# Three-slot W2 items, output projections beside attention, and queue-jumping W1 items in a fused attention and MLP kernel

## The chip, the core and the metric

The kernel runs on one core of one Trainium2 chip. The metric is device time in microseconds (us) of one execution. One timed execution varies by a few us from run to run, so times are given as medians.

The engines have short names in the profile: PE is TensorE (matmuls), PEld its weight loads, DVE is VectorE, ACT is ScalarE, SP is the engine that issues the DMAs. "L316" is line 316 of the kernel that was run; the change shifts lines, so the same statement has another number after.

## The reference, cut to what matters

```python
x  = A_x                                   # (1, 2048, 1024) bf16
xn = layernorm(x)
s  = attention(xn, A_wqkv) @ A_wo          # 32 heads of 32
y  = layernorm(xn)
h  = gelu(y @ B_w1 + B_b1)                 # (2048, 3584), tanh form of gelu
g  = silu(h @ B_w2 + B_b2)
return x + s * g
```

## The kernel before

The kernel records all operations first, with the keys that each reads and writes, and then emits one in-order stream for each engine, with a semaphore wait wherever an operation needs another engine's result. So the order in which Python records operations is the order in which an engine must execute them.

The frame is 512 "attention units": a unit is one block of 256 queries against 256 keys for four heads. In each unit ScalarE does two exponentials over 128 x 1024 values. Beside the unit TensorE runs one slot of other work, an "item", in the one PSUM bank (bank 7) that attention leaves free:

- W: a W1 item, 128 hidden features of one token chunk: 32 matmuls of 352 columns (288 in the last of six chunks),
- 2: a slot of a W2 item. A W2 item has 112 matmuls and is cut in four slots of 28,
- q, v: projections for the next head group: 32 matmuls,
- o: an output-projection item: 32 matmuls. There are 48, and what does not fit beside attention runs after it.

A W1 item gives VectorE four operations: the eviction of the bank with the bias (to `xb`), then square and cube, and, after a tanh on ScalarE for two items at once, a "gate" that writes `hT`, the input of W2. Only the eviction is recorded at once. The others stand in a list `dq`, from which each unit takes as many as a budget allows:

```python
        def later(cost, fn, lag=1):
            dq.append((cur["u"] + lag, cost, fn))

        def run_dq(budget, limit=None):     # takes from the front what fits the budget
            ...
        def hurry(cond):                    # empties the list from the front until cond holds
            while not cond():
                for v in sorted(act_tasks):
                    for t in act_tasks.pop(v):
                        t()
                run_dq(1e9, 1)

        def take(*keys):                    # a buffer is wanted again
            hurry(lambda: not busy.intersection(keys))
            busy.update(keys)
...
        # w1_item, when its matmuls are recorded (cut)
                take(kx, ku)
                op("vector", ... tensor_scalar(xb, bank(bk), b1T[:, f], op0=ALU.add), r=[("b", bk), "b1"], w=[kx])
                def square(): ...; later(0.45, cube)
                def cube():   ...; act_tasks[cur["u"] + 1].append(tanh)     # for the second of a pair
                def tanh():
                    take(kt)
                    op("scalar", ... activation(th, ut, ACT.Tanh), r=kus, w=[kt])
                    for i, (xq, kq, fq) in enumerate(pairs[m2]):
                        later(0.45, lambda ...: gate(i, xq, kq, fq), lag=0)
                def gate(i, xq, kq, fq): ...                                # hT[:, fq] = (th + 1) * xb
                    have.add((c, fq))
                later(0.45, square)
...
        # w2_item, one step: four matmuls on hT[:, f]
            def step(f, bk):
                hurry(lambda: (c, f) in have)
                op("tensor", ..., r=[("war", s, f // 4), ("hT", f)], w=[("b", bk)])
...
        NXB, NUB, NTH = 6, 2, 2      # buffers for xb, u (pairs), th (pairs)
        BUDGET = 1.25
        # the loop over units (cut)
            if u < NU: s_unit(u); exp_unit(u)        # scores, exponentials
            if 2 <= u < NU + 2: pv_unit(u - 2)       # PV and row sums
            ... the item of this unit ...
            room = BUDGET - (0.8 if ended else 0.0)
            room -= run_dq(room)
            if hi == len(it.steps):
                it.finish(state["bank"])             # records the eviction
```

`hurry` flushes the list. When a W2 slot is recorded whose `hT` is not yet produced, or when a buffer is wanted that a waiting gate still reads, everything in front of it in the list goes into VectorE's stream at that point, and the next operation of that stream waits until all of it has run.

The softmax here doesn't subtract the row's maximum and nothing guards it: scores larger than these inputs give would overflow.

Of the kernel before, what the change touches and what calls it, by code (L numbers as in the profile page):

```python
# [6 lines left out]
ACT = mybir.ActivationFunctionType  # L7
# [112 lines left out]
def bass_recurrent_scan__mha_block__mixer_channel_mlp__prompt_kernel(  # L120
# [14 lines left out]
    DC = D // 128  # L135
# [23 lines left out]
    with ExitStack() as st:  # L159
# [10 lines left out]
        iota_i = sb("iota_i", [128, 128], I32)  # L170
# [7 lines left out]
        accs = [sb(f"accs{i}", [128, QW], F32) for i in range(2)]  # L178
        trs = [sb(f"trs{i}", [128, QW], F32) for i in range(2)]
        r8s = [sb(f"r8s{i}", [128, QW // 32], F32) for i in range(2)]  # L180
        rcs = [sb(f"rcs{i}", [128, QW], F32) for i in range(2)]
# [4 lines left out]
        NXB, NUB, NTH = 6, 2, 2  # L186
        xb_t = [sb(f"xb{i}", [128, CW], F32) for i in range(NXB)]
        u_t = [sb(f"u{i}", [128, 2, CW], F32) for i in range(NUB)]
        th_t = [sb(f"th{i}", [128, 2, CW], F32) for i in range(NTH)]
# [52 lines left out]
        op("gpsimd", lambda e: e.iota(iota_i[:], pattern=[[1, 128]], base=0, channel_multiplier=-1), w=["iota"])  # L242
        op("gpsimd", lambda e: e.memset(mhalf[:], -0.5), w=["mhalf"])
        op("vector", lambda e: e.tensor_single_scalar(ident[:], iota_i[:], 0, op=ALU.is_equal), r=["iota"], w=["ident"])
# [116 lines left out]
        def later(cost, fn, lag=1):  # L361

            dq.append((cur["u"] + lag, cost, fn))

        def run_dq(budget, limit=None):
            done = 0.0
            i = 0
            while i < len(dq):
                first, cost, fn = dq[i]
                if (limit is None and first > cur["u"]) or done + cost > budget:  # L370
                    i += 1
                    if done + 0.1 > budget:
                        break
                    continue
                dq.pop(i)
                done += cost
                fn()
                if limit is not None:
                    break
            return done  # L380

        def hurry(cond):

            while not cond():
                for v in sorted(act_tasks):
                    for t in act_tasks.pop(v):
                        t()
                run_dq(1e9, 1)
# [5 lines left out]
        cur = {"u": 0}  # L394
# [37 lines left out]
        def w1_item(c, f):  # L432
# [14 lines left out]
            def fin(bk):  # L447
# [3 lines left out]
                xb, ut, th = xb_t[m % NXB], u_t[m2 % NUB], th_t[m2 % NTH]  # L451
                ub = ut[:, h, :]
                kx, ku, kt = ("xb", m % NXB), ("ub", m2 % NUB, h), ("th", m2 % NTH)
# [6 lines left out]
                def square():  # L460
                    op("vector", lambda e: e.tensor_tensor(ub[:, 0:n], xb[:, 0:n], xb[:, 0:n], op=ALU.mult), r=[kx], w=[ku])  # L461
                    later(0.45, cube)
# [8 lines left out]
                def tanh():  # L471
                    take(kt)
                    op("scalar", lambda e: e.activation(th[:, :, 0:n], ut[:, :, 0:n], ACT.Tanh, scale=0.7978845608028654 * 0.044715),  # L473
                       r=kus, w=[kt])
                    busy.difference_update(kus)
                    for i, (xq, kq, fq) in enumerate(pairs[m2]):
                        later(0.45, lambda i=i, xq=xq, kq=kq, fq=fq: gate(i, xq, kq, fq), lag=0)

                def gate(i, xq, kq, fq):
                    op("vector", lambda e: e.scalar_tensor_tensor(hT[:, fq, 0:n], th[:, i, 0:n], 1.0, xq[:, 0:n], op0=ALU.add, op1=ALU.mult),  # L480
                       r=[kt, kq], w=[("hT", fq)] + ([("xnb", i) for i in range(4)] if c == 0 else []))
                    busy.discard(kq)
                    if i == 1:
                        busy.discard(kt)
                    have.add((c, fq))
                later(0.45, square)
# [4 lines left out]
        def w2_item(c, nb):  # L491
# [36 lines left out]
            return Item([lambda bk, f=f: step(f, bk) for f in range(FB)], fin, parts=4, pre=pre)  # L528
# [3 lines left out]
        def load_res(tb):  # L532
            i4 = tb % NTB
            op("sync", lambda e: e.dma_start(xres[i4], x2[tb * 128:(tb + 1) * 128, :]), w=[("xres", i4)], dma=f"rx{i4}",
               after=[tail["xfree"]])
            lo, hi = tb * 128, (tb + 1) * 128
            cs = [c for c, (t0, n) in enumerate(chunks) if t0 < hi and t0 + n > lo]
            op("sync", lambda e: e.dma_start_transpose(gres[i4].rearrange("p (a n) -> p a n", a=1), gT_d[:, lo:hi]),
               r=[("gT", nb, c) for nb in range(DC) for c in cs], w=[("gres", i4)], dma=f"rg{i4}", after=[tail["xfree"]])
# [104 lines left out]
        for c in range(NCH):  # L644
            for f in range(FB):
                mlp.append([(w1_item(c, f), 0, DC)])
            for nb in range(DC):
                it = w2_item(c, nb)
                q = FB // it.parts
                mlp.append([(it, p * q, (p + 1) * q) for p in range(it.parts)])  # L650
# [3 lines left out]
        for hg in range(HG - 1):  # L654
# [26 lines left out]
            while len(flat) < end:  # L681
# [3 lines left out]
                if need and len(flat) >= first_proj and (late or credit >= 1):  # L685
# [15 lines left out]
        tails = mlp[mi:]  # L701
        for x in tails:
            flat += x
        for tb in range(NT):
            for k in range(len(ncol)):
                flat.append((wo_item(tb, k), 0, HG))
# [35 lines left out]
        def pv_unit(u):  # L742
# [17 lines left out]
            if kp == NKP - 1:  # L760
                g = cnt["g"]
                cnt["g"] += 1
                a, rc = accs[g % 2], rcs[g % 2]
                ka, kr = ("accs", g % 2), ("rcs", g % 2)
# [10 lines left out]
                def spread():  # L775
                    op("vector", lambda e: e.transpose(rc[:], r8[:].rearrange("p (b i) -> p b i", i=1).to_broadcast((128, QW // 32, 32))),
                       r=[kr8], w=[kr])
                    later(0.35, scale)

                def scale():  # L780
                    op("vector", lambda e: e.tensor_tensor(OT[:, hg, qb * QW:(qb + 1) * QW], a[:], rc[:], op=ALU.mult),
                       r=[ka, kr], w=[("OT", hg, qb), ("xst", 2 * hg), ("xst", 2 * hg + 1)])
                    busy.discard(ka)
                    scaled.add((hg, qb))
# [3 lines left out]
        BUDGET = 1.25  # L788
# [4 lines left out]
        while u < NU + 2 or state["qi"] < total or dq or act_tasks:  # L793
# [18 lines left out]
            if u >= NP and state["qi"] < total:  # L812
# [3 lines left out]
                it, lo, hi = entry  # L816
                for hp, which in loads.pop(qi, ()):
                    if hp < HG // 2:
                        load_wq(hp, which)
                if lo == 0:  # L820
                    if it.pre:
                        it.pre()
                    if u >= NU + 2:
                        state["bank"] = tail_banks[(tail_banks.index(state["bank"]) + 1) % len(tail_banks)]
                for fn, *a in sp_tasks.pop(u, ()):
                    fn(*a)
                for s in it.steps[lo:hi]:
                    s(state["bank"])
                room = BUDGET - (0.8 if ended else 0.0)
                room -= run_dq(room)  # L830
                if ys and (room > 0.5 or u >= 32):
                    ynorm(ys.pop(0))
                if hi == len(it.steps):
                    it.finish(state["bank"])
# [59 lines left out]
```

## Time and profile before

The median was 1132.98 us of three runs (1132.63 to 1133.45). What matters:

| | before |
|---|---|
| TensorE busy, ScalarE busy | 96%, 92% of the span |
| a unit with a W2 slot / with 32 matmuls (352 columns) | 1.92 us / 2.07 us |
| ScalarE's part of a unit | 1.83 us, and 0.57 us of tanh for two W1 items |
| TensorE waits for `hT` | 7.6 us (matmuls), 12.1 us (weight loads) |
| output projection after attention | 1088 matmuls, 39.6 us |

The first lines are from the page (busy us, share of the span, instructions), then from the waits (engine, line and tile that waited <- what it waited for: us in total, times, longest) and from the chain of waits that ended last (start us, us, what).

```profile
PE 1092.0 (96%) x29952; PEld 692.6 (61%) x29952; DVE 616.4 (54%) x1415; ACT 1046.6 (92%) x1197; POOL 24.0 (2%) x64
```
```profile
PEld ps L316 <- DVE hT L480: 12.1, 13, 2.6
PE ps L316 <- DVE hT L480: 7.6, 7, 2.3
```
```profile
953.97 10.40 DMA war<-in_B_w_dram
...
1089.44 39.61 PE ps L316 x1088
```

A matmul and its weight load wait for the same thing, so those two totals overlap and are not to be added. The DMA piece of 10.40 us is a load of MLP weights, where the median of these loads is 4.1 us. It was issued just after the 2 MB load of `wo`.

The timeline of TensorE (start us, us, engine, line, operation, tiles, count, and in brackets the idle time before and what ended it) shows an ordinary unit with a W2 slot of 28 matmuls. From one group of scores (L724) to the next it is 173.30 - 171.37 = 1.93 us:

```profile
171.37 0.40 PE L724 MATMUL ps<-QT,KT 32*128 32x256 bf16 x8
171.70 0.29 PE L753 MATMUL ps<-P,VP 128*32 128x256 bf16 x4
...
172.15 1.22 PE L316 MATMUL ps<-hT,war 128*32 128x352 bf16 x28
173.30 0.40 PE L724 MATMUL ps<-QT,KT 32*128 32x256 bf16 x8
```

Then the passage from W1 to W2 in chunk 4. The W2 slot stops after 20 matmuls for 2.19 us, until the last gates have written `hT`:

```profile
864.97 0.92 PE L316 MATMUL ps<-hT,war 128*32 128x352 bf16 x20
868.08 0.77 PE L316 MATMUL ps<-hT,war 128*32 128x352 bf16 x8 [2.19 <-DVE hT L480]
868.78 0.60 PE L724 MATMUL ps<-QT,KT 32*128 32x256 bf16 x8
...
870.14 2.25 PE L316 MATMUL ps<-hT,war 128*32 128x352 bf16 x28
872.33 0.40 PE L724 MATMUL ps<-QT,KT 32*128 32x256 bf16 x8
```

It is not VectorE that is full here. It stood idle for 4.00 us before these gates, because the tanh that they read came late on ScalarE, behind a row of exponentials:

```profile
861.14 5.66 ACT L736 ACTIVATE P<-ps 128x1024 bf16<-128x1024 f32 x6
866.56 0.91 ACT L473 ACTIVATE th<-u 128x704 f32<-128x704 f32 x1
867.50 0.96 DVE L480 SCALAR_TENSOR_TENSOR hT<-th,xb 128x352 bf16<-128x352 f32 x2 [4.00 <-ACT th L473]
```

The built order shows how the list leads there. The last two cubes were still in the list when the W2 slot was recorded, `hurry` then recorded the tanh after that unit's two exponentials, and the gates after the tanh. The stops near 164, 691 and 1004 us look the same.

The windows of one us (for each window the busy us of the engines, then the granted clock of TensorE, the DMA share and GB/s):

```profile
867.00:868.00 1.00, 0.00 (x0) 0.00 (x0) 0.50 (x2) 0.47 (x1) 0.00 (x0) 1.00 0.91 274
868.00:869.00 1.00, 0.81 (x16) 0.34 (x16) 0.56 (x3) 0.00 (x0) 0.00 (x0) 0.92 0.14 42
869.00:870.00 1.00, 1.00 (x24) 0.53 (x20) 0.49 (x1) 0.56 (x1) 0.00 (x0) 0.50 0.06 16
870.00:871.00 1.00, 1.00 (x20) 0.58 (x16) 0.00 (x0) 1.00 (x2) 0.00 (x0) 0.50 0.00 0
871.00:872.00 1.00, 1.00 (x20) 0.49 (x12) 0.15 (x1) 0.76 (x2) 0.00 (x0) 0.50 0.00 0
872.00:873.00 1.00, 1.00 (x30) 0.46 (x26) 0.37 (x1) 0.22 (x1) 0.00 (x0) 0.88 0.00 0
```

### The profile page before, as it was taken

To read this page: it belongs to the slowest core of one execution; us is meant where nothing else is said; L and a number is where in the kernel's file an instruction comes from. 1 tells how busy PE (TensorE), PEld (TensorE's weight loads), DVE (VectorE), ACT (ScalarE), POOL (GpSimd) and SP (SyncE) were. 2 spreads that over 40 slices of the span, in tenths; PEclk is the share of its full clock that TensorE was granted. 3 is DMA by queue.
4 is the path that set the end of the run, shared out by engine and by line. 5 is a ranking of instruction groups with operands and counts; after the bars stand their busy time and mean duration, and the time that the engine had idled before them with its cause. 6 is when DMAs were issued, how large, how long until landed. Compare 5 with 4: busy or idle time off the path is not lost.

```text
span 1133.6 us, 63287 instructions
## 1 busy us (share of the span) xinstructions
PE 1092.0 (96%) x29952; PEld 692.6 (61%) x29952; DVE 616.4 (54%) x1415; ACT 1046.6 (92%) x1197; POOL 24.0 (2%) x64
## 2 busy tenths in 40 slices
PE   5999999999999999999999999999999999989998
PEld 4856656666666666665566655666655665656666
DVE  8457862266663237774237663246574246842378
ACT  4899999999999999999999999999998999989930
POOL 4300000000000000000000000000000000000000
PEclk9999999999999999999999999999999999989999
DMA  9233545323316404324522327431234435534677
GB/s 233 68 105 110 185 112 164 115 62 97 96 40 156 128 23 138 106 78 115 144 89 78 105 77 173 127 96 48 78 105 110 120 95 167 160 92 125 118 174 170
DMA packets 202420, 129.93 MB, mean 115 GB/s; under 512 B 45488, under 2 KB 192944, under 8 KB 202160
## 3 DMA queue, kind: packets, MB, share of 16 engines
q1 hardware_dynamic: 197520, 125.86, 39.6%
q8 instruction: 234, 3.83, 1.4%
q0 software_dynamic: 4640, 0.02, 0.6%
q14 instruction: 26, 0.21, 0.1%
HBM read 104.87 MB, written 12.58 MB: 104 GB/s over the span
## 4 chain that ended last, share of the span: by engine, by line
PE 53%; ACT 42%; DVE 2%; DMA 2%; issue 1%; SPq 0%; POOL 0%; DVEq 0%
ACT P L736 37%; PE ps L316 31%; PE ps L724 9%; PE ps L753 8%; PE ps L756 5%; ACT th L473 4%; DMA war<-in_B_w_dram 1%; DVE stats L253 1%; DMA xnT<-gT_scratch 0%; PE ps L307 0%; DVE hT L480 0%; ACT thz L518 0%; DMA OT<-in_A_x_dram 0%; DVE wq L564 0%; DVE hT L285 0%
## 5 line engine op out<-in xcount | busy, mean ns | idle before, releaser
L736 ACT ACTIVATE P<-ps 128x1024 bf16<-128x1024 f32 x1024 | 967.6, 1076 | 21.1 <-PE ps L724 14.8
L753 PE MATMUL ps<-P,VP 128*32 128x256 bf16 x4096 | 262.9, 279 | 0.0
L756 PE MATMUL ps<-P,ones 128*32 128x256 bf16 x4096 | 257.8, 274 | 0.0
L316 PE MATMUL ps<-hT,war 128*32 128x352 bf16 (+1 forms) x5376 | 233.2, 311 | 9.5 <-DVE hT L480 7.6
L316 PE MATMUL ps<-yTc,war 128*32 128x352 bf16 (+1 forms) x5376 | 226.1, 309 | 3.0 <-issue 1.2
L724 PE MATMUL ps<-QT,KT 32*128 32x256 bf16 x4096 | 204.7, 274 | 12.9 <-ACT P L736 7.7
L753 PEld LDWEIGHTS ps<-P,VP 128*32 128x32 bf16 x4096 | 107.6, 95 | 111.1 <-issue 104.9
L316 PEld LDWEIGHTS ps<-hT,war 128*32 128x32 bf16 x5376 | 141.5, 98 | 54.8 <-DVE hT L480 11.3
L316 PEld LDWEIGHTS ps<-yTc,war 128*32 128x32 bf16 x5376 | 138.6, 97 | 50.0 <-issue 1.8
L455 DVE TENSOR_SCALAR xb<-ps,b1T 128x352 f32<-128x352 f32 (+1 forms) x168 | 96.2, 572 | 124.3 <-PE ps L316 124.1
L724 PEld LDWEIGHTS ps<-QT,KT 32*128 32x128 bf16 x4096 | 60.9, 92 | 157.8 <-ACT P L736 98.8
L316 PE MATMUL ps<-xnT,wq 128*32 128x352 bf16 (+2 forms) x3200 | 129.5, 305 | 2.6 <-DMA wq<-in_A_wqkv_dram 1.4
L756 PEld LDWEIGHTS ps<-P,ones 128*32 128x32 bf16 x4096 | 109.2, 96 | 1.3
L514 DVE TENSOR_SCALAR zh<-ps,b2h 128x352 f32<-128x352 f32 (+1 forms) x48 | 27.5, 573 | 137.6 <-PE ps L316 137.6
L316 PEld LDWEIGHTS ps<-xnT,wq 128*32 128x32 bf16 x3200 | 80.5, 97 | 30.2 <-DMA wq<-in_A_wqkv_dram 1.7
L480 DVE SCALAR_TENSOR_TENSOR hT<-th,xb 128x352 bf16<-128x352 f32 (+1 forms) x168 | 82.3, 505 | 24.8 <-ACT th L473 24.4
L465 DVE SCALAR_TENSOR_TENSOR u<-u,xb 128x352 f32<-128x352 f32 (+1 forms) x168 | 83.7, 504 | 0.0
L461 DVE TENSOR_TENSOR u<-xb 128x352 f32<-128x352 f32 (+1 forms) x168 | 83.4, 503 | 0.3
L768 DVE COPY accs<-ps 128x256 f32<-128x256 f32 x64 | 27.2, 424 | 78.4 <-PE ps L756 78.3
L473 ACT ACTIVATE th<-u 128x704 f32<-128x704 f32 (+1 forms) x84 | 67.7, 805 | 0.4 <-DVE u L465 0.4
L316 PE MATMUL ps<-wq,xnT 128*32 128x256 bf16 x2048 | 65.6, 273 | 0.9 <-DMA wq<-in_A_wqkv_dram 0.6
L316 PE MATMUL ps<-xnT,OT 128*32 128x352 bf16 (+1 forms) x1536 | 58.0, 308 | 0.5 <-DVE wq L564 0.5
(44 smaller groups left out, 463.5 us busy)
## 6 DMA issues: line engine op xcount, KB each, us to landing
war<-in_B_w_dram SPq DMA_DIRECT2D x336, 256.0 KB, 4.1
wq<-in_A_wqkv_dram SPq DMA_DIRECT2D x12, 512.0 KB, 4.9
OT<-in_A_x_dram SPq DMA_DIRECT2D x16, 256.0 KB, 7.6
y_scratch<-OT SPq DMA_DIRECT2D x16, 256.0 KB, 3.3
xnT<-in_A_x_dram SPq DMA_DIRECT2D x16, 256.0 KB, 4.2
out_dram<-wq SPq DMA_DIRECT2D x16, 256.0 KB, 2.6
gT_scratch<-gst SPq DMA_DIRECT2D x40, 88.0 KB, 1.7
xnT<-in_A_wo_dram SPq DMA_DIRECT2D x1, 2048.0 KB, 10.0
```

The costliest lines, as they stand in the source:

```text
L316: ins = e.matmul(outs(j), lhsT=lhs(j), rhs=rhs, start=start, stop=stop, tile_position=(0, 32 * j), skip_group_check=True)
L455: op("vector", lambda e: e.tensor_scalar(xb[:, 0:n], bank(bk, 0, n), b1T[:, f:f + 1], None, op0=ALU.add), r=[("b", bk), "b1"], w=[kx])
L461: op("vector", lambda e: e.tensor_tensor(ub[:, 0:n], xb[:, 0:n], xb[:, 0:n], op=ALU.mult), r=[kx], w=[ku])
L465: op("vector", lambda e: e.scalar_tensor_tensor(ub[:, 0:n], ub[:, 0:n], 1.0 / 0.044715, xb[:, 0:n], op0=ALU.add, op1=ALU.mult), r=[kx, ku] ...
L473: op("scalar", lambda e: e.activation(th[:, :, 0:n], ut[:, :, 0:n], ACT.Tanh, scale=0.7978845608028654 * 0.044715), r=kus, w=[kt])
L480: op("vector", lambda e: e.scalar_tensor_tensor(hT[:, fq, 0:n], th[:, i, 0:n], 1.0, xq[:, 0:n], op0=ALU.add, op1=ALU.mult), r=[kt, kq], w= ...
L514: op("vector", lambda e: e.tensor_scalar(zh[:, 0:n], bank(bk, 0, n), 0.25, b2h[:, nb:nb + 1], op0=ALU.mult, op1=ALU.add), r=[("b", bk), "b ...
L724: ins = e.matmul(bank(bks[j], kh * 256, (kh + 1) * 256), lhsT=KT[i2][32 * j:32 * j + 32, k0:k0 + 128], rhs=QT[i2][32 * j:32 * j + 32, qb * ...
L736: op("scalar", lambda e, p=p, sl=sl: e.activation(pb[:, 2 * p:2 * p + 2, :, :].rearrange("p a b q -> p (a b q)"), ps[:, sl * 1024:(sl + 1) ...
L753: e.matmul(bankq(ACC, j, 0, QW), lhsT=VP[vp][:, kb, vo + 32 * j:vo + 32 * j + 32], rhs=pb[:, j, kh, :], start=first, stop=False, tile_posi ...
L756: ins = e.matmul(bankq(ACC, j, QW, 2 * QW), lhsT=ones[:, 0:32], rhs=pb[:, j, kh, :], start=False, stop=last, tile_position=(0, 32 * j), sk ...
L768: op("vector", lambda e: e.tensor_copy(a[:], bank(ACC, 0, QW)), r=[("b", ACC)], w=[ka])
```

## The change

Its intent: fill the attention units better, so that less output projection is left for the end, and keep VectorE's backlog from stopping TensorE where W1 goes over to W2. Its parts:

1. W2 items of chunks 0 to 2 in three slots (40, 36, 36 matmuls; "dense slots" from here on) instead of four: 24 slots are saved.
2. Output-projection items may stand among the last attention units.
3. The VectorE operations of a chunk's last eight W1 items go to the front of the list ("queue-jumping").
4. More buffers (eight `xb`, four `u`; the tanh is written in place, the room comes from `th`, `rcs` and `iota`), and a budget of 1.35 in place of 1.25, which fits three operations of 0.45 instead of two.
5. Some projection items are held back for the change from W1 to W2 ("placing").

The diff, cut to its core:

```diff
-        NXB, NUB, NTH = 6, 2, 2
+        NXB, NUB = 8, 4
-        def later(cost, fn, lag=1):
-            dq.append((cur["u"] + lag, cost, fn))
+        def later(cost, fn, lag=1, first=False):
+            if first:
+                dq.insert(cur["front"], (cur["u"] + lag, cost, fn))
+                cur["front"] += 1
+            else:
+                dq.append((cur["u"] + lag, cost, fn))
 ...
+                soon = f >= FB - 8
-                    later(0.45, cube)
+                    later(0.45, cube, lag=0 if soon else 1, first=soon)
-                    take(kt)
-                    op("scalar", lambda e: e.activation(th[:, :, 0:n], ut[:, :, 0:n], ACT.Tanh, ...), r=kus, w=[kt])
+                    op("scalar", lambda e: e.activation(ut[:, :, 0:n], ut[:, :, 0:n], ACT.Tanh, ...), r=kus, w=kus)
-                        later(0.45, lambda ...: gate(i, xq, kq, fq), lag=0)
+                        later(0.45, lambda ...: gate(i, xq, kq, fq), lag=0, first=soon)
-                later(0.45, square)
+                later(0.45, square, first=soon)
 ...
-            return Item([...], fin, parts=4, pre=pre)
+            return Item([...], fin, parts=4 if c >= 3 else 3, pre=pre)
 ...
-                if need and len(flat) >= first_proj and (late or credit >= 1):
+                keep = 2 if len(mlp[mi]) == 1 and any(len(x) > 1 for x in mlp[mi:mi + left - need]) else 0
+                change = mi and len(mlp[mi - 1]) == 1 and len(mlp[mi]) > 1
+                if need and len(flat) >= first_proj and (late or change or (credit >= 1 and need > keep)):
 ...
-        tails = mlp[mi:]
-        for x in tails:
-            flat += x
-        for tb in range(NT):
-            for k in range(len(ncol)):
-                flat.append((wo_item(tb, k), 0, HG))
+        rest = mlp[mi:]
+        wos = [(tb, k) for tb in range(NT) for k in range(len(ncol))]
+        while rest or wos:
+            u = len(flat) + NP
+            if wos and (wos[0][0] < 6 or not rest) and u >= (HG - 1) * UPH + NKP * (wos[0][0] // 2 + 1) + 8:
+                flat.append((wo_item(*wos.pop(0)), 0, HG))
+            elif rest:
+                flat += rest.pop(0)
+            else:
+                flat.append(None)
 ...
-        BUDGET = 1.25
+        BUDGET = 1.35
```

More of the change, by code (lines that the diff above doesn't have):

```diff
@@ L169, in bass_recurrent_scan__mha_block__mixer_channel_mlp__prompt_kernel @@
         ident = sb("ident", [128, 128], BF16)
-        iota_i = sb("iota_i", [128, 128], I32)
         ones = sb("ones", [128, 32], BF16)
@@ L178, in bass_recurrent_scan__mha_block__mixer_channel_mlp__prompt_kernel @@
         accs = [sb(f"accs{i}", [128, QW], F32) for i in range(2)]
+        iota_i = accs[0][:, 0:128].bitcast(I32)
         trs = [sb(f"trs{i}", [128, QW], F32) for i in range(2)]
         r8s = [sb(f"r8s{i}", [128, QW // 32], F32) for i in range(2)]
-        rcs = [sb(f"rcs{i}", [128, QW], F32) for i in range(2)]
         hT = sb("hT", [128, FB, CW], BF16)
@@ L185, in bass_recurrent_scan__mha_block__mixer_channel_mlp__prompt_kernel @@
         wq = sb("wq", [128, 3, DC, 256], BF16)
-        NXB, NUB, NTH = 6, 2, 2
+        NXB, NUB = 8, 4
         xb_t = [sb(f"xb{i}", [128, CW], F32) for i in range(NXB)]
         u_t = [sb(f"u{i}", [128, 2, CW], F32) for i in range(NUB)]
-        th_t = [sb(f"th{i}", [128, 2, CW], F32) for i in range(NTH)]
         zh_t = [sb(f"zh{i}", [128, CW], F32) for i in range(2)]
@@ L241, in bass_recurrent_scan__mha_block__mixer_channel_mlp__prompt_kernel @@
             load_x(tb)
-        op("gpsimd", lambda e: e.iota(iota_i[:], pattern=[[1, 128]], base=0, channel_multiplier=-1), w=["iota"])
+        op("gpsimd", lambda e: e.iota(iota_i, pattern=[[1, 128]], base=0, channel_multiplier=-1), w=["iota"])
         op("gpsimd", lambda e: e.memset(mhalf[:], -0.5), w=["mhalf"])
-        op("vector", lambda e: e.tensor_single_scalar(ident[:], iota_i[:], 0, op=ALU.is_equal), r=["iota"], w=["ident"])
+        op("vector", lambda e: e.tensor_single_scalar(ident[:], iota_i, 0, op=ALU.is_equal), r=["iota"], w=["ident"])
         op("vector", lambda e: e.memset(ones[:], 1.0), w=["ones"])
@@ L375, in run_dq @@
                 dq.pop(i)
+                if i < cur["front"]:
+                    cur["front"] -= 1
                 done += cost
@@ L384, in hurry @@
             while not cond():
+                assert dq or act_tasks
                 for v in sorted(act_tasks):
@@ L392, in take @@
             busy.update(keys)
-        cur = {"u": 0}
+        cur = {"u": 0, "front": 0}
         cnt = {"w1": 0, "w2": 0, "piece": 0, "g": 0, "wo": 0, "store": 0}
@@ L450, in fin @@
                 h, m2 = m % 2, m // 2
-                xb, ut, th = xb_t[m % NXB], u_t[m2 % NUB], th_t[m2 % NTH]
+                xb, ut = xb_t[m % NXB], u_t[m2 % NUB]
                 ub = ut[:, h, :]
-                kx, ku, kt = ("xb", m % NXB), ("ub", m2 % NUB, h), ("th", m2 % NTH)
+                kx, ku = ("xb", m % NXB), ("ub", m2 % NUB, h)
+                soon = f >= FB - 8
                 take(kx, ku)
@@ L471, in tanh @@
                 def tanh():
-                    take(kt)
-                    op("scalar", lambda e: e.activation(th[:, :, 0:n], ut[:, :, 0:n], ACT.Tanh, scale=0.7978845608028654 * 0.044715),
-                       r=kus, w=[kt])
-                    busy.difference_update(kus)
+                    op("scalar", lambda e: e.activation(ut[:, :, 0:n], ut[:, :, 0:n], ACT.Tanh, scale=0.7978845608028654 * 0.044715),
+                       r=kus, w=kus)
                     for i, (xq, kq, fq) in enumerate(pairs[m2]):
-                        later(0.45, lambda i=i, xq=xq, kq=kq, fq=fq: gate(i, xq, kq, fq), lag=0)
+                        later(0.45, lambda i=i, xq=xq, kq=kq, fq=fq: gate(i, xq, kq, fq), lag=0, first=soon)
                 def gate(i, xq, kq, fq):
-                    op("vector", lambda e: e.scalar_tensor_tensor(hT[:, fq, 0:n], th[:, i, 0:n], 1.0, xq[:, 0:n], op0=ALU.add, op1=ALU.mult),
-                       r=[kt, kq], w=[("hT", fq)] + ([("xnb", i) for i in range(4)] if c == 0 else []))
-                    busy.discard(kq)
-                    if i == 1:
-                        busy.discard(kt)
+                    op("vector", lambda e: e.scalar_tensor_tensor(hT[:, fq, 0:n], ut[:, i, 0:n], 1.0, xq[:, 0:n], op0=ALU.add, op1=ALU.mult),
+                       r=[kus[i], kq], w=[("hT", fq)] + ([("xnb", i) for i in range(4)] if c == 0 else []))
+                    busy.difference_update((kq, kus[i]))
                     have.add((c, fq))
-                later(0.45, square)
+                later(0.45, square, first=soon)
                 if f == FB - 1 and c + 1 < NCH:
@@ L527, in fin @@
                 act_tasks[u + 2].append(tanh)
-            return Item([lambda bk, f=f: step(f, bk) for f in range(FB)], fin, parts=4, pre=pre)
+            return Item([lambda bk, f=f: step(f, bk) for f in range(FB)], fin, parts=4 if c >= 3 else 3, pre=pre)
         tail = {}
@@ L536, in load_res @@
             lo, hi = tb * 128, (tb + 1) * 128
+            assert all(("gT", nb, NCH - 1) in pg.lastw for nb in range(DC)) or hi <= chunks[-1][0]
             cs = [c for c, (t0, n) in enumerate(chunks) if t0 < hi and t0 + n > lo]
@@ L648, in bass_recurrent_scan__mha_block__mixer_channel_mlp__prompt_kernel @@
                 it = w2_item(c, nb)
-                q = FB // it.parts
-                mlp.append([(it, p * q, (p + 1) * q) for p in range(it.parts)])
+                cut = [-(-FB * p // it.parts) for p in range(it.parts + 1)]
+                mlp.append([(it, lo, hi) for lo, hi in zip(cut, cut[1:])])
         flat = []
@@ L762, in pv_unit @@
                 cnt["g"] += 1
-                a, rc = accs[g % 2], rcs[g % 2]
-                ka, kr = ("accs", g % 2), ("rcs", g % 2)
+                a, ka = accs[g % 2], ("accs", g % 2)
                 tr, r8 = trs[g % 2], r8s[g % 2]
@@ L775, in spread @@
                 def spread():
-                    op("vector", lambda e: e.transpose(rc[:], r8[:].rearrange("p (b i) -> p b i", i=1).to_broadcast((128, QW // 32, 32))),
-                       r=[kr8], w=[kr])
+                    op("vector", lambda e: e.transpose(tr[:], r8[:].rearrange("p (b i) -> p b i", i=1).to_broadcast((128, QW // 32, 32))),
+                       r=[kr8], w=[ktr])
                     later(0.35, scale)
                 def scale():
-                    op("vector", lambda e: e.tensor_tensor(OT[:, hg, qb * QW:(qb + 1) * QW], a[:], rc[:], op=ALU.mult),
-                       r=[ka, kr], w=[("OT", hg, qb), ("xst", 2 * hg), ("xst", 2 * hg + 1)])
+                    op("vector", lambda e: e.tensor_tensor(OT[:, hg, qb * QW:(qb + 1) * QW], a[:], tr[:], op=ALU.mult),
+                       r=[ka, ktr], w=[("OT", hg, qb), ("xst", 2 * hg), ("xst", 2 * hg + 1)])
                     busy.discard(ka)
@@ L815, in bass_recurrent_scan__mha_block__mixer_channel_mlp__prompt_kernel @@
                 state["qi"] += 1
-                it, lo, hi = entry
-                for hp, which in loads.pop(qi, ()):
-                    if hp < HG // 2:
-                        load_wq(hp, which)
-                if lo == 0:
-                    if it.pre:
-                        it.pre()
-                    if u >= NU + 2:
-                        state["bank"] = tail_banks[(tail_banks.index(state["bank"]) + 1) % len(tail_banks)]
-                for fn, *a in sp_tasks.pop(u, ()):
-                    fn(*a)
-                for s in it.steps[lo:hi]:
-                    s(state["bank"])
-                room = BUDGET - (0.8 if ended else 0.0)
-                room -= run_dq(room)
-                if ys and (room > 0.5 or u >= 32):
-                    ynorm(ys.pop(0))
-                if hi == len(it.steps):
-                    it.finish(state["bank"])
+                if entry:
+                    it, lo, hi = entry
+                    for hp, which in loads.pop(qi, ()):
+                        if hp < HG // 2:
+                            load_wq(hp, which)
+                    if lo == 0:
+                        if it.pre:
+                            it.pre()
+                        if u >= NU + 2:
+                            state["bank"] = tail_banks[(tail_banks.index(state["bank"]) + 1) % len(tail_banks)]
+                    for fn, *a in sp_tasks.pop(u, ()):
+                        fn(*a)
+                    for s in it.steps[lo:hi]:
+                        s(state["bank"])
+                    room = BUDGET - (0.8 if ended else 0.0)
+                    room -= run_dq(room)
+                    if ys and (room > 0.5 or u >= 32):
+                        ynorm(ys.pop(0))
+                    if hi == len(it.steps):
+                        it.finish(state["bank"])
+                else:
+                    run_dq(BUDGET)
                 if state["qi"] == q_end:
```

## The prediction

> **What bounds the kernel now.** The work is 512 attention units; beside each, TensorE runs one "item" (a W1, projection or output-projection item: 32 matmuls; a W2 item cut in four slots of 28). The chain of waits shows a unit's price on TensorE: scores 0.33 us, PV and sums about 0.55 us, 28 matmuls 1.04 us, 32 matmuls 1.19 us: 1.92 us for a W2 slot, 2.07 us with 32 matmuls. (The Trainium skill, "TensorE: Matmul & The Clock Gate", Back-to-back issue gap: N/2.4 + 2.5 ns, so 149 ns per group of four column tiles of N = 352, 1.19 us for 32; the trace agrees.) ScalarE's share of a unit is 1.83 us (two exponentials of 0.916 us in the chain), plus 0.57 us of tanh per two W1 items. Both are nearly full (page: PE 96%, ACT 92%); TensorE bounds most units. At the end, 34 output-projection items run on TensorE alone: 1088 matmuls in 39.6 us, 1.165 us each.
>
> By the starts of units in the timeline, units 8 to 511 take 1025.5 us; their prices add up to 999. Of the 27 us over, about 21 are stalls: where W1 goes over to W2, TensorE waits for the last gate operations that stand behind a VectorE backlog (hT from L480; units of 4.8, 4.6, 4.6+3.6 and 5.1+3.2+2.8 us, some 17 us over price), and a wait of some 3.3 us near 958 us for war, whose loads queue behind the 2 MB load of wo (a 10.4 us DMA piece in the chain).
>
> **What the change does.** Built, it has 518 item slots instead of 540.
> - Three slots for W2 of chunks 0 to 2: 24 slots fewer, but 40 or 36 matmuls each: about 2.27 us by the prices, 6.8 us per item against 7.68.
> - Output-projection items beside attention: 36 instead of 12; 12 remain alone: 24 x 1.165 = 28 us off the tail. But those units now cost about 2.07 us, so the prices of units 8 to 511 rise from 999 to 1026.5 us. The two almost cancel.
> - Last eight W1 items first in VectorE's queue, more xb and u buffers, a budget of three operations, and projection items kept for the change of stage: in the built order the last gates stand one to several units ahead of the W2 slot that reads them, except in chunk 1 (zero). I expect 15 to 17 us of stalls to go: the real gain.
> - wo now loads among W2 pieces: a stall of 0 to 3 us can stay.
>
> **Estimate.** Attention: 1026.5 + some 11 us of remainder (27 now), 12 us longer than before; tail 28 us shorter. Net -16 us: **1117 us**, range 1109 to 1125. Faster by over 2%: 0.15; within 2%: 0.83; slower by over 2%: 0.02.
>
> **What would show it.** The timeline: W2 units of chunks 0 to 2 of 2.2 to 2.4 us; the last scores begin about 12 us later; about 12 items alone, 14 us of unbroken matmuls, at the end. The waits: PE/PEld on hT (L480 before) from about 20 us to under 4. Windows: ScalarE idle 0.3 us per unit in dense W2 stages. Page: PE's share up to 97 or 98%.
>
> **What would make it wrong.** A dense slot that costs more than its prices (weights not landed in the shorter item); the output projection's transposing loads stalling in mid-attention; VectorE late with evictions in the 14-item W1 run.

The 149 ns and the 1.19 us in the bracket are an estimate from the skill's formula, which the page gives for an isolated matmul. The 1.19 us in the sum itself was read from the trace.

## The result, and the profile after

The changed kernel took 1123.58 us in the median of four runs (1121.87 to 1125.11), the kernel before 1133.22 us. Ratios here are the mean time of one kernel's fast runs over that of the other's of the same rounds, so they are not quite the ratio of the medians. This one is 0.9912 (95% interval 0.9893 to 0.9932): within 2%, some 10 us less. The prediction said 1117 us, 1109 to 1125. A second set of six runs later (run e5 below) gave 1121.34 us and 0.9891 (0.9870 to 0.9911).

The page and the waits of the changed kernel:

```profile
PE 1085.4 (97%) x29952; PEld 692.4 (62%) x29952; DVE 621.5 (55%) x1415; ACT 1053.0 (94%) x1197; POOL 24.0 (2%) x64
```
```profile
PEld ps L314 <- DVE xb L461: 4.7, 8, 2.6
PE ps L314 <- DVE xb L461: 2.7, 2, 2.3
```

No wait of the item matmuls (now L314) on `hT` is left: 19.7 us as the profile counts them for both queues have become zero. In their place stands a wait on `xb` (L461, the eviction of the item bank), which was 1.2 us on the matmuls before.

The timeline of the dense slots shows 40 and 36 matmuls, and units of 317.44 - 315.22 = 2.22 us for 36:

```profile
313.62 1.67 PE L314 MATMUL ps<-hT,war 128*32 128x352 bf16 x40
315.22 0.40 PE L733 MATMUL ps<-QT,KT 32*128 32x256 bf16 x8
...
316.00 1.52 PE L314 MATMUL ps<-hT,war 128*32 128x352 bf16 x36
317.44 0.40 PE L733 MATMUL ps<-QT,KT 32*128 32x256 bf16 x8
```

The end is shorter, by the chain: 320 matmuls in 11.96 us alone where there were 1088 in 39.61.

```profile
1103.49 11.96 PE ps L314 x320
```

**The balance.** The starts of the scores in the timeline give each unit's length, and the built order tells what item it holds. I price a unit at 0.88 us for scores, PV and sums, plus 0.0373 us for each item matmul of 352 columns (0.0340 for 320, 0.0310 for 288, 0.0335 for v), and at no less than the 1.83 us of ScalarE. These prices are estimates from the groups of the trace of before. "Over" is what units 8 to 510 took beyond their prices; "tail" runs from the scores of unit 511 to the end of the last matmul. One execution each, the profiled one:

| | prices | measured | over | tail |
|---|---|---|---|---|
| before | 996.7 | 1025.5 | 28.8 | 45.3 |
| after | 1024.5 | 1039.5 | 15.0 | 17.7 |
| change | +27.8 | +14.0 | -13.8 | -27.6 |

So the dense slots and the shorter tail cancel to 0.2 us, and the gain is the part over price. (My count in the prediction was one unit off. The scores of one unit near 552 us were recorded in two groups, so "27 us over" is really 28.8.) The profiled run of after is also one of its faster ones, 1121.87 us, and that of before one of its slower ones, 1135.39 us. The difference of these two profiles is therefore larger than that of the medians.

**What the changed kernel lost.** Near 957 us, in the run of W1 items of the last chunk, the chain reads as follows ("issue" is time in which an engine waited for nothing that the profile shows):

```profile
956.97 0.57 ACT u L478
957.54 0.02 issue
957.57 1.21 DVE hT L484 x3
...
958.87 0.53 DVE xb L461
959.40 0.04 issue
959.44 1.38 PE ps L314 x32
```

and the timeline of TensorE, which stood still meanwhile:

```profile
956.19 0.40 PE L733 MATMUL ps<-QT,KT 32*128 32x256 bf16 x8
...
959.44 1.38 PE L314 MATMUL ps<-xnT,wq 128*32 128x352 bf16 x32 [2.30 <-DVE xb L461]
```

The built order of unit 440 explains it. VectorE gets, ahead of the eviction into `xb` buffer 6: cube, square, cube, the gates of features 24 and 25, and then the gate of feature 18. Feature 18 is just too early to jump, so the jumping operations of features 20 to 25 had overtaken it. It still held `xb` buffer 6, which the new item wanted, and `take` emptied the list from the front to get at it. The gates wait for a tanh, the tanh for its turn among the exponentials, and the eviction stands behind them. The Trainium skill, "PSUM — Partial Sum Buffer", "Engine vs sequencer instructions", says that "ScalarE/VectorE/GpSimdE queues are strict FIFO". The trace agrees: the item's matmuls were over by about 956.2 us, and the eviction began at 958.87 us. The next item needs the same bank.

The unit with this stop took 2.5 us over price. More went to three other units, near 446, 920 and 1023 us, which stopped at "issue" and took some 4 us over price together. The longest of these stops cuts a group of scores in two, and its cause stays open:

```profile
1025.11 0.29 PE L733 MATMUL ps<-QT,KT 32*128 32x256 bf16 x3 [1.62 <-issue]
```

**The clock.** The ten runs of the changed kernel (both sets) fall in two groups by their mean granted clock. The four at 1.000 took 1119.1 to 1122.5 us (mean 1120.8), the six at 0.995 to 0.998 took 1121.3 to 1126.2 (mean 1124.0). The kernel before ran mostly at 0.993 to 0.995, and took 1130 to 1133 us in the few runs at 0.997 or 0.998.

### The profile page after: what moved, and what is told of

It reads as the page before. It is cut to its first block, busy times and chain, and to the rows that moved or that the text cites. A ratio compares the mean times of both kernels' runs of the same rounds, so it can differ in the third digit from the quotient of the medians.

```text
span 1120.0 us, 63277 instructions
## 1 busy us (share of the span) xinstructions
PE 1085.4 (97%) x29952; PEld 692.4 (62%) x29952; DVE 621.5 (55%) x1415; ACT 1053.0 (94%) x1197; POOL 24.0 (2%) x64
## 4 chain that ended last, share of the span: by engine, by line
PE 52%; ACT 43%; DVE 2%; DMA 1%; issue 1%; SPq 1%; DVEq 0%
ACT P L745 38%; PE ps L314 31%; PE ps L733 8%; PE ps L762 8%; PE ps L765 5%; ACT u L478 4%; DMA wq<-in_A_wqkv_dram 1%; DVE hT L484 1%; ACT thz L520 0%; PE ps L305 0%; SPq L223 0%; ACT xnT L308 0%; DMA xnT<-gT_scratch 0%; DVE xb L461 0%; DVE wq L567 0%
## 5 line engine op out<-in xcount | busy, mean ns | idle before, releaser
L314 PE MATMUL ps<-hT,war 128*32 128x352 bf16 (+1 forms) x5376 | 224.6, 308 | 0.5 <-issue 0.5
L314 PE MATMUL ps<-yTc,war 128*32 128x352 bf16 (+1 forms) x5376 | 224.1, 308 | 1.0 <-issue 0.7
L314 PEld LDWEIGHTS ps<-hT,war 128*32 128x32 bf16 x5376 | 141.7, 97 | 42.5 <-issue 1.2
L314 PEld LDWEIGHTS ps<-yTc,war 128*32 128x32 bf16 x5376 | 137.1, 97 | 47.7 <-DVE VP L350 1.4
L461 DVE TENSOR_SCALAR xb<-ps,b1T 128x352 f32<-128x352 f32 (+1 forms) x168 | 96.1, 572 | 111.7 <-PE ps L314 111.1
L314 PE MATMUL ps<-xnT,wq 128*32 128x352 bf16 (+2 forms) x3200 | 129.7, 305 | 4.7 <-DVE xb L461 2.3
L314 PEld LDWEIGHTS ps<-xnT,wq 128*32 128x32 bf16 x3200 | 81.7, 97 | 31.2 <-DVE xb L461 2.9
L484 DVE SCALAR_TENSOR_TENSOR hT<-u,xb 128x352 bf16<-128x352 f32 (+1 forms) x168 | 80.5, 507 | 14.0 <-ACT u L478 13.5
L478 ACT ACTIVATE u<-u 128x704 f32<-128x704 f32 (+1 forms) x84 | 68.0, 809 | 0.0
L314 PE MATMUL ps<-wq,xnT 128*32 128x256 bf16 x2048 | 66.3, 274 | 1.2 <-ACT xnT L308 0.6
L314 PE MATMUL ps<-xnT,OT 128*32 128x352 bf16 (+1 forms) x1536 | 62.4, 308 | 0.8 <-DVE wq L567 0.8
```

The costliest lines, as they stand in the source:

```text
L314: ins = e.matmul(outs(j), lhsT=lhs(j), rhs=rhs, start=start, stop=stop, tile_position=(0, 32 * j), skip_group_check=True)
L461: op("vector", lambda e: e.tensor_scalar(xb[:, 0:n], bank(bk, 0, n), b1T[:, f:f + 1], None, op0=ALU.add), r=[("b", bk), "b1"], w=[kx])
L478: op("scalar", lambda e: e.activation(ut[:, :, 0:n], ut[:, :, 0:n], ACT.Tanh, scale=0.7978845608028654 * 0.044715), r=kus, w=kus)
L484: op("vector", lambda e: e.scalar_tensor_tensor(hT[:, fq, 0:n], ut[:, i, 0:n], 1.0, xq[:, 0:n], op0=ALU.add, op1=ALU.mult), r=[kus[i], kq] ...
```

## The experiments

Twelve runs, in three sets, each beside the kernel before on the same chip. The theories: **A**, the prediction's, the gain is the stalls at the change from W1 to W2, and dense slots only move work; **B**, the dense slots and the shorter tail make the gain.

| run | what | median us | ratio to before (95%) | over | tail |
|---|---|---|---|---|---|
| e1 | change without dense slots, projection last | 1127.30 | 0.9946 (0.9929 to 0.9963) | 19.8 | 45.3 |
| e2 | dense slots and projection alone | 1130.26 | 0.9971 (0.9950 to 0.9991) | 25.1 | 17.7 |
| e3 | no queue-jumping | 1119.88 | 0.9882 (0.9858 to 0.9905) | 11.9 | 17.7 |
| e4 | no placing of projection items | 1119.12 | 0.9872 (0.9854 to 0.9890) | 12.4 | 17.7 |
| e5 | the change again | 1121.34 | 0.9891 (0.9870 to 0.9911) | 12.1 | 17.7 |
| e6 | four items jump, not eight | 1118.82 | 0.9861 (0.9848 to 0.9873) | 12.2 | 17.5 |
| e7 | e6, dense in chunks 1, 2, 5 | 1121.99 | 0.9888 (0.9874 to 0.9902) | 16.8 | 17.5 |
| e8 | e7, no placing | 1119.52 | 0.9865 (0.9850 to 0.9879) | 15.9 | 17.5 |
| e9 | no dense slots, no flush, budget of four | 1125.58 | 0.9931 (0.9919 to 0.9944) | 18.6 | 45.5 |
| e10 | e9, `wo` loaded later | 1126.10 | 0.9936 (0.9924 to 0.9948) | 19.5 | 45.3 |
| e11 | dense in 1, 2, 5, no flush, budget of four | 1118.98 | 0.9879 (0.9863 to 0.9895) | 11.1 | 17.8 |
| e12 | e6 with a budget of four | 1122.24 | 0.9903 (0.9889 to 0.9917) | 16.1 | 17.8 |

Prices of units 8 to 510 are 996.7 us without dense slots (e1, e9, e10), 1024.5 us with them in chunks 0 to 2, 1021.9 us in chunks 1, 2 and 5. "Over" is from the profiled execution alone, the median from all.

### e1: the queue part alone

```diff
-            return Item([...], fin, parts=4 if c >= 3 else 3, pre=pre)
+            return Item([...], fin, parts=4, pre=pre)
-            if wos and (wos[0][0] < 6 or not rest) and u >= ...
+            if wos and not rest and u >= ...
```

> The change with W2 in four slots in every chunk and the output projection strictly last (540 slots, 36 items after attention, as before); buffers, VectorE order, budget and the placing of projection items stay changed. Theory A (the prediction: the gain is the stalls at the change from W1 to W2, dense slots only move work): most of the gain is here, about 1119 to 1123 us; some 4 to 6 us short of the 16 predicted, because here the wo load still falls among the W1 loads and the last chunk has twenty W1 items in a row. Rival B (dense slots and the shorter tail make the gain): 1130 to 1134 us. The waits: TensorE on hT under 3 us in both.

Measured 1127.3 us, between the two ranges; neither theory had it. The waits on `hT` are gone, as was expected under both theories. But a larger flush of the kind above came in:

```profile
PEld ps L314 <- DVE xb L461: 9.3, 11, 3.7
PE ps L314 <- DVE xb L461: 6.1, 5, 3.4
```

Here the last chunk has twenty W1 items in a row, and in units 462 and 464 the order puts nine and eight VectorE operations between one eviction and the next. Four units near 974 to 990 us took 8.3 us over price, and the granted clock was 0.50 from 980 to 984 us. Two more units, where weights wait behind the load of `wo`, took 2.9 us over.

### e2: dense slots and the output projection alone

```diff
 # the kernel before, with only:
-            return Item([...], fin, parts=4, pre=pre)
+            return Item([...], fin, parts=4 if c >= 3 else 3, pre=pre)
 # and the new loop over rest and wos (as in the change)
```

> The kernel before with only W2 of chunks 0 to 2 in three slots and output-projection items among the last attention units (518 slots, 12 items after attention); buffers, order and budget as before. Theory A: 1129 to 1134 us, the tail 28 us shorter and attention 25 to 28 us longer, waits of TensorE on hT still about 20 us. Rival B: 1120 to 1125 us.

Measured 1130.26 us, in A's range, though still faster than before by some 3 us. The tail is 27.6 us shorter and the prices 27.8 us higher: they cancel. The waits on `hT` are as large as before:

```profile
PEld ps L316 <- DVE hT L480: 13.2, 14, 2.5
PE ps L316 <- DVE hT L480: 9.0, 9, 2.2
```

The 3.7 us less over price lie in the last chunk: its 28 W1 items took 7.0 us over price in the trace of before and 3.3 us here. The stall for `wo` (3.3 us in the trace of before) is absent, as `wo` is issued at 984.7 us here, among W2 items. These are single profiles. e1 and e2 together make 6.1 + 3.3 = 9.4 us by their ratios (0.54% and 0.29% of 1134 us), close to the 10 us that the whole change made in its first set (12.4 us in its second).

### e3 and e4: which part of the queue work removes the stalls

```diff
 # e3
-                soon = f >= FB - 8
+                soon = False
 # e4
-                if need and len(flat) >= first_proj and (late or change or (credit >= 1 and need > keep)):
+                if need and len(flat) >= first_proj and (late or credit >= 1):
```

> The changed kernel with no queue-jumping (the last eight W1 items line up like the others). In the built order the last gates still stand ahead of the W2 slot that reads them, by 1 to 14 units (0 in chunk 1), and no gate is flushed for a buffer at the end of the last chunk. If queue-jumping removed the stalls: 1130 us or more. If the buffers, the budget and the placing removed them: the same as the changed kernel, or 2 us less, as the wait of 2.6 us on xb near 957 us (gates pushed behind the jumping ones, then flushed together) goes.

> The changed kernel with projection items placed as before (none kept for the change of stage). The last gates stand 0 to 3 units ahead of their readers in the built order. If the placing matters: TensorE waits for hT of 3 us or more and 1126 us or more; if buffers and budget suffice: within 2 us of the changed kernel.

e3 took 1119.88 us and e4 1119.12 us. Neither the jumping nor the placing is needed as long as the other stays: with one of them removed the kernel is not slower than the change (0.9882 and 0.9872 against 0.9912 in the first set and 0.9891 in the second, intervals that partly overlap). No run lacks both, so it is open whether one of them must be there. In e3 one wait on `hT` of 2.0 us came back, in chunk 1, where the order leaves no distance; the wait on `xb` fell to 0.2 us. In e4 the flush is gone too (longest wait on `xb` 0.7 us), because in the built order, with the items placed otherwise, no gate is flushed. What remains common to e3, e4 and the change are the buffers and the budget of three operations. That these suffice is likely, but not shown: buffers and budget were not run alone.

### e5 and e6: the flush

e5 is the change again. e6 alters one number:

```diff
-                soon = f >= FB - 8
+                soon = f >= FB - 4
```

> The changed kernel itself, unaltered, as the measure for the three below on the same chip: 1121 to 1126 us, the runs at a mean clock of 1.000 some 2 to 3 us shorter than those at 0.998.

> The changed kernel with four W1 items of a chunk jumping VectorE's queue instead of eight; nothing else changes. In the built order no gate is flushed for a buffer any more (before: six operations ahead of one bank eviction in unit 440). If that flush costs what the trace shows (TensorE idle 2.6 us on xb near 957 us): 2 to 4 us less than the changed kernel of the same call, and no wait on xb over 1 us. If the flush only hides another wait: no difference.

e5 took 1121.34 us (1119.09 to 1126.15), e6 1118.82 us (1118.32 to 1119.40), 2.5 us less in the median and 3.4 us in the mean, in the range that was expected for the flush. The wait on `xb` in e5, and then both waits in e6:

```profile
PE ps L314 <- DVE xb L461: 2.1, 2, 1.7
```
```profile
PEld ps L314 <- DVE xb L461: 1.0, 3, 0.7
PE ps L314 <- DVE xb L461: 0.4, 1, 0.4
```

The spread went as well: e6 ran at a clock of 0.999 or 1.000 in all four runs, e5 at 0.995 to 1.000. "Over" in the two profiles is equal (12.1 and 12.2), because the profiled run of e5 was one at full clock and e6 had small stops elsewhere. The gain therefore shows in the timed runs, not in one profile, and it is tied to the clock: e5's two runs at 1.000 took 1119.09 and 1119.82 us, in the mean 0.6 us above e6's, and the rest comes from its four runs at a lower clock. The intervals of the two ratios overlap a little. That the lower clock in those runs follows this very stop is likely, but not shown: the profiled runs of the change were at 1.000.

### e7 and e8: dense slots where ScalarE bounds

```diff
 # e7: e6 with
-            return Item([...], fin, parts=4 if c >= 3 else 3, pre=pre)
+            return Item([...], fin, parts=3 if c in (1, 2, 5) else 4, pre=pre)
 # e8: e7 with the placing undone as in e4
```

> As the run before, but the W2 items in three slots are those of chunks 1, 2 and 5 instead of 0, 1 and 2; slots and items after attention are the same in number (518, 12). By the unit prices dense slots gain nothing where TensorE bounds (352 columns: four slots 7.68 us, three 6.8, and the freed slot is filled), but in the last chunk (288 columns) ScalarE bounds four slots at about 7.6 us against 6.1 in three: 2.6 to 4.6 us less than the run before, less whatever the wo load costs now that it falls before the last W1 to W2 change (up to 3 us). If dense slots are worth the same anywhere: no difference.

> The run before without the placing of projection items at the change of stage. The last gates stand at least 2 units ahead of their readers in chunks 0 to 4 with or without it, so: within 2 us of the run before. If the placing matters: 3 us or more longer.

e7 missed: 1121.99 us, 3.2 us more than e6 where 2.6 to 4.6 less were expected. The gain in the prices (2.6 us) is there, but 4.6 us were added over them. At the last change from W1 to W2 the gates of features 21 to 23 had been overtaken in their turn and were flushed in the W2 slot:

```profile
PEld ps L314 <- DVE hT L484: 2.8, 2, 2.5
PE ps L314 <- DVE hT L484: 2.2, 1, 2.2
```

That slot and the next took 4.2 us over price, with the clock at 0.59 from 980 to 984 us, and a W1 unit near 968 us 1.6 us more. e8 took 1119.52 us, 2.5 us less than e7, just outside "within 2 us". Its VectorE order at the last change from W1 to W2 is the same as in e7, and so is the stop:

```profile
978.56 1.16 PE L314 MATMUL ps<-hT,war 128*32 128x288 bf16 x24 [2.19 <-DVE hT L484]
```

Here the clock stayed at 1.00 after it, where in e7 it fell to 0.59. A second stop, of 2.7 us on the first output-projection item, was followed by a slow unit. So the flush alone does not explain why e7 is slower than e6, and the difference between e7 and e8 is left unexplained: their mean clocks are the same, 0.997 to 0.998.

### e9 to e12: a queue without a flush, with a budget of four

```diff
 # all four
-                soon = f >= FB - 8
+                soon = f >= FB - 4
-        BUDGET = 1.35
+        BUDGET = 1.8
 # e9, e10: no dense slots, projection last (as e1). e11: dense in chunks 1, 2, 5
 # e10: wo is loaded 22 units later, e11: 6 units later
                 if state["qi"] == q_end:
                     tail["xfree"] = pg.lists["tensor"][-1]
+                if state["qi"] == q_end + 22:
                     op("sync", lambda e: e.dma_start(wo_sb, ...), w=["wo"], dma="wo", after=[tail["xfree"]])
```

> W2 in four slots everywhere, the output projection strictly last (540 slots, 36 items after attention), and VectorE's queue without a flush: four W1 items jump, budget for four queued operations; in the built order the last gates stand 2 units or more ahead everywhere and no unit queues seven or more operations. If dense slots and the shorter tail are worth nothing by themselves, this is as fast as the run with four jumping items and dense slots (1119 us) but for the wo load among the W1 loads (2.9 us in the first run of this kind): 1119 to 1123 us. If they are worth 3 us or more beyond that load: 1124 us or more.

> As the run before, but wo is loaded 22 units later, when the W1 loads are through. If the wo load stalls the W1 items by queueing ahead of their weights: 2 to 4 us less than the run before, no stretched unit near 950 us, and level with dense slots (1117 to 1120 us). If not: no difference.

> Dense slots in chunks 1, 2 and 5 with the same queue (four jump, budget of four; last gates at least 1 unit ahead, no unit with seven operations) and wo loaded 6 units later, among W2 loads. If dense slots pay where ScalarE bounds the four-slot form (last chunk) and nothing else is lost: 1113 to 1117 us, 2 to 5 us less than the next run. If the first try of this (1122 us) was slow for dense slots themselves and not for its flush and its wo load: 1119 us or more.

> The changed kernel (dense slots in chunks 0 to 2) with four W1 items jumping and a budget of four: the last gates stand at least 1 unit ahead also in chunk 1. Against the run with four jumping items and budget 1.35 (1118.8 us): the same, within 1.5 us; if VectorE is too full with four operations in a unit, 3 us or more longer, with waits on xb.

e12 against e6 tests the budget. By ratio it is slower, 0.9903 against 0.9861, with intervals that do not meet, though in different sets. TensorE waited for evictions 22 times on its weight loads, 0.3 us each in the mean, against three times in e6. That VectorE was too full with four operations in a unit is what this suggests.

```profile
PEld ps L314 <- DVE xb L461: 6.7, 22, 0.5
```

The units with such a wait took 4.8 us over price in e12 and 0.3 us in e6 (3.6, 4.3 and 6.2 us in e11, e10 and e9). So all four runs carry such a cost, and are to be compared among themselves. e9 against e12 (no dense slots against dense slots, same queue, same set): 1125.58 and 1122.24 us. Dense slots, with the output projection that they let in beside attention, are worth 3.3 us beyond the cancelling terms. The balance of the two profiles says where. The 28 W1 items of the last chunk took 8.6 us over price in e9 and 3.5 us in e12. Without dense slots they come late, twenty in a row with no projections left between them, and a row of W1 items asks 1.83 + 0.57/2 = 2.12 us of ScalarE where TensorE needs 0.88 + 32 x 0.0310 = 1.87 us. Dense slots in early chunks bring this chunk forward, among the projections. About 2.8 us of the 8.6 is the stall behind the load of `wo`.

e10 missed: the later load of `wo` changed nothing (1126.10 us). In its profile the two units near 955 us are no longer stretched, but others are, near 964 and 998 us, by 1.8 and 1.4 us. The first of these the trace puts down to nothing ("issue", 1.13 us). What the load costs by itself stays open.

e11 against e12, in the same set: 1118.98 and 1122.24 us, 3.3 us less, in the range of 2 to 5. With the flush out of the way, dense slots in the last chunk gain, as the prices have it (2.6 us). e11 also loads `wo` 6 units later, which was not tried alone; 22 units changed nothing in e10. In four slots, TensorE's price there is 0.88 + 28 x 0.0310 = 1.75 us and ScalarE's 1.83 us, and the units in the trace of the changed kernel are mostly 1.83 us long. In absolute time it missed 1113 to 1117 us, for the budget's cost. Dense slots in chunks 1, 2 and 5 with the budget of three and no flush were not run.

The lowest ratio is that of e6: 1118.82 us, 0.9861 of the kernel before. The intervals of e3, e4, e8 and e11 overlap with its own, so which of them is fastest is not shown.

## Why the prediction was right or wrong

The prediction held: 1123.58 us lies in 1109 to 1125, and within 2% had a chance of 0.83. Its centre was 6.6 us too low. Point by point:

- *"Dense slots ... the two almost cancel."* Right, by +27.8 and -27.6 us in the balance and by e2. What it left out is that the saved slots also bring the last chunk forward, worth 3.3 us (e9 against e12), the `wo` stall included. So dense slots do not only move work.
- *"Attention ... 12 us longer than before; tail 28 us shorter."* 14.0 and 27.6 us in the profiles.
- *"the last gate operations that stand behind a VectorE backlog."* Half right. The list made the tanh and the gates late, but before these gates VectorE stood idle for 1.57 to 4.43 us, waiting for a tanh behind exponentials on ScalarE.
- *"PE/PEld on hT from about 20 us to under 4."* Right: to zero.
- *"About 12 items alone, 14 us of unbroken matmuls."* 320 matmuls, ten items, unbroken in 11.96 us; the others stand between the last PV groups and evictions.
- *"W2 units of 2.2 to 2.4 us."* Right: 2.22 and 2.37 us. *"ScalarE idle 0.3 us per unit"* there was 0.2 us: in 315 to 365 us ScalarE was busy 45.57 of 50 us, over 22 units.
- *"PE's share up to 97 or 98%"*: 97%.
- *"VectorE late with evictions in the 14-item W1 run"*, named as what could go wrong: the mechanism came, in another place. It was not the long run of items with three operations each (2.07 to 2.08 us per unit there, but for one of 2.39). It was one flush in the last chunk, which the queue-jumping itself made.

The step that failed in size is *"some 11 us of remainder (27 now)"*, that is, the stalls to go. Over price there remained 15.0 us (12.1 in the second profile) of 28.8. Three things were left out. The first is the flush, 2.5 us over price in the first profile (1.9 in the second). One number in e6 removed it, and that kernel took 1118.82 us, within 2 us of the forecast. The second is the stops at "issue", some 4 us in the first profile. The third is the clock, which shows in the timed runs: both profiles ran at 1.000. I had read the long units after a stall as waiting too ("4.6+3.6", "5.1+3.2+2.8"), but the second and third units are slow matmuls at half clock. A stop thus costs more than its own length, and not in every run; six of ten runs of the changed kernel ran at a lower mean clock, 3.2 us slower in the mean.

The profiles themselves differ by 13.6 us by the balance, where 16 were forecast. Most of the rest of the 6.6 us lies in the base: the forecast took 16 us off the median, but had worked them out on a profiled run of before that was 2.2 us above its median, and the profiled run of after is 1.7 us below its own.

I also credited the jumping and the placing with the gain. e3 and e4 show that neither is needed while the other stays. The forecast had put all the queue work into one term, so its number could hold although not every part of it was needed.

## What to carry to other kernels

Moving work between stages that the same engine bounds gains nothing, however much shorter the tail looks; add up that engine's prices before and after, and look at the part over price. In an in-order queue a priority is paid by what it overtakes: if an overtaken operation holds a buffer, a later request for that buffer flushes everything in front of it, ahead of the one operation that TensorE waits for. A full engine can be hurt by short stops twice, by the stop and by the slower clock after it: in the kernel before, the unit after a stop of 2.19 us took 1.6 us over price, while after a stop of 2.26 us the clock stayed full. And when an engine waits for the last operation of a list, look one step further back: in the kernel before VectorE was idle too (for 4.00 us at the stop shown), waiting for ScalarE.

## What the Trainium skill lacked or had wrong

- "TensorE: Matmul & The Clock Gate", "HAM oscillation — how this bites in real kernels" gives the rule "no PE-idle gaps >~3.4µs". Here shorter stops sufficed. In the kernel before, a stop of 2.19 us (to 868.08 us) was followed by a clock of 0.50 from about 868.8 to 872.2 us; in e4 a stop of 1.96 us (to 1005.31 us) by 0.70 and 0.88 in the windows from 1004 to 1008 and to 1012 us. It is not certain either: a stop of 2.26 us (to 166.76 us) in the kernel before left the clock at 1.00, and a stop of 2.19 us was followed by 0.59 in e7 and by 1.00 in e8. That the window runs free, as the page's Part 1 says, fits this.
- The same page, section "Back-to-back issue gap", agrees where the prediction used it (1.19 us for 32 column-tiled matmuls of 352 columns within attention); alone in the tail 22 items of 352 and 12 of 320 columns took 39.61 us, where the formula gives an estimate of 39.3 us. The page says of this formula that at large N it over-counts in a stream of matmuls (its figures are for N = 512); at 352 and 320 columns, in groups of four column tiles, it did not.
- No page that I read prices what a full in-order VectorE queue costs TensorE through a single item bank: with four queued operations for each unit instead of three there were 22 waits of about 0.3 us (e12) instead of three waits (e6).
